# Loading alpha ahead of x, and moving the w_in transposes into the first fills

## The chip, the cores and the metric

The kernel runs on one core of a Trainium2 chip. The metric is the device time in microseconds (us).

## The reference

Two stages follow each other. First an attention block: 32 inducing vectors attend to x (4 batches of 12480 tokens, 128 channels), which gives h; x then attends to h. Then a feed-forward layer with a leaky ReLU that has one slope for each hidden unit:

```python
h = mab(I, x)                 # softmax attention of 32 vectors over 12480 tokens
x = mab(x, h)                 # (4 * 12480, 128)
h = x @ w_in                  # 128 -> 2048
g = np.maximum(h, 0.0) + alpha * np.minimum(h, 0.0)
out = g @ w_out               # 2048 -> 128
```

## The kernel before

The leaky ReLU is split into a ReLU part, with the weights W1 = (1 - alpha) * w_out, and a linear part that needs only the 128 x 128 matrix Amat = w_in @ (alpha * w_out). So alpha is needed to make W1 and AW = alpha * w_out on GpSimd, and w_in must be transposed once (two calls of `w_inT`, eight transposes each) for Amat.

A *fill* is the kernel's unit of steady work: four matmuls `ring<-rep,hW`, four evictions with ReLU to `gt` by ACT or DVE, and sixteen matmuls `acc<-W,gt`. Before the first fill there is a *head* that loads batch 0, transposes x on PE, and computes h. A planner in the kernel chooses for each fill which of ACT and DVE evicts which bank; extra work is given to a slot (group, step) of the fills with `at(...)`.

The head, with cuts. `pin` keeps the program order on an engine; `bank()` takes the next of six PSUM banks.

```python
ind_f = const.tile([M, C], f32, name="ind_f")
nc.sync.dma_start(out=ind_f[:], in_=inducing)
xs = const.tile([P, NQ, GRP], f32, name="xs")           # first block of x
pin(nc.sync.dma_start(out=xs[:, 0:2, :], in_=src[:, 0:2, :]))      # SP half
pin(nc.scalar.dma_start(out=xs[:, 2:4, :], in_=src[:, 2:4, :]))    # ACT half
for u in order[1:3]:
    a_load(st, u, pieces=2)                             # GpSimd queue, casts to bf16
make_identity(nc, ident[:]); make_identity(nc, ident32[:])
al_f = const.tile([KC, P], f32, name="al_f")
nc.sync.dma_start(out=al_f[:], in_=moe_alpha.rearrange("(k p) -> k p", p=P))
for u in order[3:]:
    a_load(st, u, pieces=2)
...                                                     # w_in, w_out on the GpSimd queue
nc.tensor.transpose(alp[:, :KC], al_f[:], ident32[:KC, :KC])
nc.vector.tensor_copy(out=alT[:], in_=alp[:, :KC])
nc.vector.tensor_scalar(out=om_al[:], in0=alT[:], ...)  # 1 - alpha
...
def warm(n):                                            # n transposes that nobody reads
    ...
pin(nc.vector.tensor_copy(out=xn0[:, 0:2, :], in_=xs[:, 0:2, :]))  # the cast of the SP half
pin(nc.scalar.copy(out=xn0[:, 2:4, :], in_=xs[:, 2:4, :]))
a_xpose_pe(st, order[0])                                # PE transposes of x
for i in range(n - 1):
    a_xpose_pe(st, order[i + 1])
    ...                                                 # e1 transposes, scores, accumulation
h_sum(st); w_scale(W1, om_al); w_scale(AW, alT)
...
h_den(st)
w_inT(0)
a_accum(st, order[n - 1], pool)
...                                                     # h, hW, then the fills
at(0, lambda: w_inT(KC // 2), 3, (460, "A", 960))
at(1, w_amat, 1, (950, "D", 250))
```

The softmax here doesn't subtract the row's maximum and nothing guards it: scores larger than these inputs give would overflow.

Of the kernel before, what the change touches and what calls it, by code (L numbers as in the profile page):

```python
# [11 lines left out]
MULT = mybir.AluOpType.mult  # L12
ADD = mybir.AluOpType.add
AXX = mybir.AxisListType.X

P = 128
# [8 lines left out]
def kernel(  # L25
# [9 lines left out]
    nc = tc.nc  # L35
    f32 = mybir.dt.float32
# [12 lines left out]
    KC = DFF // P  # L49
# [38 lines left out]
    def bank():  # L88
        t = ring[ring_n[0] % RING]
        ring_n[0] += 1  # L90
        return t
# [57 lines left out]
    def a_xpose_pe(st, u):  # L149
        xn = st.xn[u]  # L150
        if u < NS:
            for i in range(2):
                tp = bank()[:].bitcast(bf16)
                for k in range(2 * NB):
                    q, j = 2 * i + k // NB, k % NB
                    pin(nc.tensor.transpose(
                        tp[:, k * P : (k + 1) * P], xn[:, q, j * C : (j + 1) * C], ident[:]
                    ))
                dst = st.xT[:, u, 2 * i : 2 * i + 2, :].rearrange("c q t -> c (q t)")
                if i == 0 or u == order[-1]:  # L160
                    pin(nc.vector.tensor_copy(out=dst, in_=tp))
                else:
                    pin(nc.scalar.copy(out=dst, in_=tp))
        else:
            tp = bank()[:].bitcast(bf16)
            for j in range(JR):
                pin(nc.tensor.transpose(
                    tp[:, j * PR : (j + 1) * PR], xn[:, j, :], ident[:PR, :PR]
                ))
            pin(nc.vector.tensor_copy(  # L170
                out=st.xTr[:].rearrange("c j p -> c (j p)"), in_=tp[:, :REM]
            ))

    def e_xpose_pe(st, u):
        e1 = st.e1.pop(u)
        tp = bank()[:].bitcast(bf16)
        if u < NS:
            e1T = work.tile([P, NB, P], bf16, name="e1T", tag="e1T")
            for j in range(NB):
                pin(nc.tensor.transpose(  # L180
                    tp[:, j * P : (j + 1) * P], e1[:, j * P : (j + 1) * P], ident[:]
                ))
            pin(nc.vector.tensor_copy(
                out=e1T[:].rearrange("p j m -> p (j m)"), in_=tp[:, : NB * P]
            ))
        else:
            e1T = work.tile([P, JR, M], bf16, name="e1Tr", tag="e1Tr")
            for j in range(JR):
                pin(nc.tensor.transpose(
                    tp[:PR, j * M : (j + 1) * M], e1[:, j, :PR], ident[:M, :M]  # L190
                ))
            pin(nc.vector.tensor_copy(
                out=e1T[:PR].rearrange("p j m -> p (j m)"), in_=tp[:PR, : JR * M]
            ))
        st.e1T[u] = e1T

    def a_scores(st, u, by_dma=True):
        ps = bank()
        if u < NS:
            for q in range(NQ):  # L200
                mm(ps[32 * q : 32 * q + 32, :], IT[:], st.xT[:, u, q, :])
            e1 = work.tile([P, GRP], bf16, name="e1", tag="e1")
            pin(nc.scalar.activation(
                out=e1[:], in_=ps[:], func=EXP, scale=scale, accum_out=st.es[:, u : u + 1]
            ))
            if by_dma:
                e1T = work.tile([P, NB, P], bf16, name="e1T", tag="e1T")
                pin(nc.sync.dma_start_transpose(out=e1T[:], in_=e1[:]))
        else:
            mm(ps[0:M, :REM], IT[:], st.xTr[:].rearrange("c j p -> c (j p)"))  # L210
            e1 = e1r
            pin(nc.scalar.activation(
                out=e1[:, :, :PR],
                in_=ps[0:M, :REM].rearrange("m (j p) -> m j p", j=JR),
                func=EXP, scale=scale, accum_out=st.es[0:M, u : u + 1],
            ))
            if by_dma:
                e1T = work.tile([P, JR, M], bf16, name="e1Tr", tag="e1Tr")
                pin(nc.sync.dma_start_transpose(
                    out=e1T[:], in_=e1[:].rearrange("m j p -> m (j p)")  # L220
                ))
        if by_dma:
            st.e1T[u] = e1T
        else:
            st.e1[u] = e1
# [3 lines left out]
    def a_accum(st, u, into=None, first=False):  # L229
        xn = st.xn.pop(u)  # L230
        e1T = st.e1T.pop(u)
        alone = into is None
        ps = bank() if alone else into
        if u < NS:
            for j in range(NB):
                for q in range(NQ):
                    mm(
                        ps[32 * q : 32 * q + 32, :C],
                        e1T[:, j, 32 * q : 32 * q + 32],
                        xn[:, q, j * C : (j + 1) * C],  # L240
                        start=(j == 0 and (alone or first)), stop=(j == NB - 1),
                        skip_group_check=not alone,
                    )
            if alone:
                pin(nc.vector.tensor_tensor(
                    out=st.hacc[:], in0=ps[:, :C], in1=st.hacc[:], op=ADD
                ))
        else:
            for j in range(JR):
                mm(  # L250
                    ps[0:M, :C], e1T[:PR, j, :], xn[:, j, :],
                    start=(j == 0 and alone), stop=(j == JR - 1),
                    skip_group_check=not alone,
                )
            if alone:
                pin(nc.vector.tensor_tensor(
                    out=st.hacc[0:M, :], in0=ps[0:M, :C], in1=st.hacc[0:M, :], op=ADD
                ))
# [212 lines left out]
    st = new_batch(0)  # L471
    ind_f = const.tile([M, C], f32, name="ind_f")
    nc.sync.dma_start(out=ind_f[:], in_=inducing)


    xs = const.tile([P, NQ, GRP], f32, name="xs")
# [6 lines left out]
    make_identity(nc, ident[:])  # L483
    ident32 = const.tile([P, P], f32, name="ident32")
    make_identity(nc, ident32[:])
    al_f = const.tile([KC, P], f32, name="al_f")
    nc.sync.dma_start(out=al_f[:], in_=moe_alpha.rearrange("(k p) -> k p", p=P))
    for u in order[3:]:
        a_load(st, u, pieces=2)
    w_in_b = const.tile([C, DFF], bf16, name="w_in_b")  # L490
# [10 lines left out]
    for q in range(4):  # L501
# [13 lines left out]

    e1r = const.tile([M, JR, P], bf16, name="e1r")
    nc.vector.memset(e1r[:], 0.0)
    alp = bank()
    alT = const.tile([P, KC], f32, name="alT")
    nc.tensor.transpose(alp[:, :KC], al_f[:], ident32[:KC, :KC])  # L520
    nc.vector.tensor_copy(out=alT[:], in_=alp[:, :KC])
    om_al = const.tile([P, KC], f32, name="om_al")
    nc.vector.tensor_scalar(
        out=om_al[:], in0=alT[:], scalar1=-1.0, scalar2=1.0, op0=MULT, op1=ADD
    )
    W1 = const.tile([P, KC, C], bf16, name="W1")
    AW = const.tile([P, KC, C], bf16, name="AW")
    winT = const.tile([P, KC, C], bf16, name="winT")
    Amat = const.tile([C, C], bf16, name="Amat")


    def w_scale(dst, fac):
        for j in range(NJ):
            f = fac[:, j::NJ]
            fb = bass.AP(tensor=f.tensor, offset=f.offset, ap=[f.ap[0], f.ap[1], [0, C]])
            pin(nc.gpsimd.tensor_tensor(
                out=dst[:, j::NJ, :], in0=w_out_f[:, j::NJ, :], in1=fb, op=MULT
            ))
# [7 lines left out]
    def w_inT(k0):  # L546
        wtp = bank()[:].bitcast(bf16)
        for k in range(8):
            pin(nc.tensor.transpose(
                wtp[:, k * P : (k + 1) * P],  # L550
                w_in_b[:, (k0 + k) * P : (k0 + k + 1) * P], ident[:],
            ))
        pin(nc.scalar.copy(
            out=winT[:, k0 : k0 + 8, :].rearrange("p k c -> p (k c)"), in_=wtp
        ))
# [15 lines left out]

    pool = accs[0][:, 0, :]
    n = len(order)
    a_xpose_pe(st, order[0])
    for i in range(n - 1):
        a_xpose_pe(st, order[i + 1])
        if i > 0:
            e_xpose_pe(st, order[i - 1])
        a_scores(st, order[i], by_dma=False)
        if 0 < i < n - 2:  # L580
            a_accum(st, order[i - 1], pool, i == 1)
    a_scores(st, order[n - 1], by_dma=False)
    e_xpose_pe(st, order[n - 2])
    a_accum(st, order[n - 3], pool)
    h_sum(st)
    w_scale(W1, om_al)
    w_scale(AW, alT)
    e_xpose_pe(st, order[n - 1])
    a_accum(st, order[n - 2], pool)
    h_den(st)  # L590
    w_inT(0)
    a_accum(st, order[n - 1], pool)
    pin(nc.vector.tensor_copy(out=st.hacc[:], in_=pool))
    warm(6)
# [13 lines left out]
    def at(slot, fn, j=1, cost=None):  # L608
        tasks.setdefault((slot, j), []).append((fn, cost))
# [5 lines left out]
    for q in range(1, NQ):  # L615
        at(0, lambda q=q: b_scores_pe(st, 0, q), q, (240, "A", 480))
    at(1, lambda: b_den_pe(st, 0, 0), 0, (130, "D", 250))
    at(0, lambda: w_inT(KC // 2), 3, (460, "A", 960))
    at(1, w_amat, 1, (950, "D", 250))
    at(1, lambda: h_linear(st), 2, (80, "D", 250))  # L620
# [151 lines left out]
```

## Time and profile before

| | before |
|---|---|
| median time, 3 runs | 597.71 us (597.15 to 598.29) |
| span of the profiled run (an execution of 598.94 us) | 597.2 us |
| SP half of x: issued, landed | 1.20, 6.21 us |
| first x transpose on PE | 8.00 us |
| clock records: full TensorE clock from | 14.53 us |
| last x piece landed | 19.87 us |
| first fill | 28.47 us |

The page of the kernel before; part 1 (busy time, share, instructions) and part 4 (the chain that ended last):

```profile
...
PE 582.9 (98%) x9186; PEld 435.0 (73%) x9186; DVE 518.6 (87%) x878; ACT 507.1 (85%) x994; POOL 84.9 (14%) x170
...
PE 58%; ACT 0%; DVE 0%; issue 0%
...
```

PE is busy nearly all the time, and the chain runs through PE. So what the head loses or gains at the first fill is passed on to the end.

The DVE timeline of the head (start us, duration us, engine, line, operation, tiles):

```profile
...
6.89 0.17 DVE L521 COPY alT<-ring_82 128x16 f32<-128x16 f32 x1 [2.72 <-PE ring_82 L520]
7.10 0.17 DVE L523 TENSOR_SCALAR om_al<-alT 128x16 f32<-128x16 f32 x1
7.18 0.76 DVE L568 CAST xn<-xs 128x1024 bf16<-128x1024 f32 x1
9.07 0.69 DVE L161 COPY xT<-ring_83 128x1024 bf16<-128x1024 bf16 x1 [1.13 <-PE ring_83 L156]
...
```

The cast of x (L568) starts at 7.18, right behind the two alpha instructions. Its data were there earlier, as the view of the tile `xs` shows: the SP queue issued the half at 1.2 us, and the longer of the two landings (the SP half's) took 5.0 us.

```profile
...
L478 SPq DMA_DIRECT2D xs<-in_x_dram x1: 409/409/409, 1.2 to 1.2; - x1
...
DMA to landing us min/median/max: 4.0/4.5/5.0
```

The PE timeline of the head and of the first fill:

```profile
...
6.59 0.26 PE L520 MATMUL ring_82<-ident_110,al_f 16*128 16x16 f32 x1 [2.64 <-DMA al_f<-in_moe_alpha_dram]
8.00 1.04 PE L156 MATMUL ring_83<-ident,xn 128*128 128x128 bf16 x8 [1.14 <-DVE xn L568]
8.82 1.06 PE L156 MATMUL ring_84<-ident,xn 128*128 128x128 bf16 x8
...
14.76 0.62 PE L156 MATMUL ring_85<-ident,xn 128*128 128x128 bf16 x8
...
21.38 0.61 PE L156 MATMUL ring_86<-ident,xn 128*128 128x128 bf16 x8
...
24.80 0.38 PE L94 MATMUL ring_86<-et,fold 128*128 128x1 f32 x2
25.05 0.61 PE L549 MATMUL ring_81<-ident,w_in_b 128*128 128x128 bf16 x8
25.58 0.41 PE L94 MATMUL acc_87<-xn,e1T 128*32 128x128 bf16 x16
...
28.47 0.39 PE L94 MATMUL ring_85<-rep,hW 32*128 32x512 bf16 x1
...
```

Eight x transposes take 1.04 us at first and 0.62 us from 14.76 on: in the trace they start every 107 ns, then every 56 ns. The eight w_in transposes (L549) stand before the last accumulation (25.58).

The table by stretch (length, then busy us of PE, PEld, DVE, ACT, POOL, then clock, DMA share, GB/s) shows the first fills:

```profile
...
30.00:35.00 5.00, 5.00 (x71) 3.65 (x71) 4.47 (x8) 4.80 (x9) 5.00 (x6) 1.00 0.01 3
...
```

In these 5 us PE has no idle time, ACT 0.20 us and DVE 0.53 us. The page's clock column cannot be used for the head: it shows 1.00 where the trace holds no clock record. The switch times in this text come from the trace's clock records, which say from when to when a full or a half clock was granted; they agree with the spacing of the transposes.

### The profile page before, as it was taken

What the parts mean: (1) busy time and instruction counts of PE and PEld (TensorE: products, weight loads), DVE (VectorE), ACT (ScalarE), POOL (GpSimd) and SP (SyncE); (2) the same over time, 40 slices, a digit from 0 to 9 for tenths busy, and PEclk for the clock granted to TensorE, in tenths of its full rate; (3) what the DMA queues carried; (4) which work ended last, traced back from release to release, by engine and by line L of the source; (5) the groups of instructions that cost most, each with busy time, mean ns of one, the idle gap of its engine ahead of it and who ended that gap; (6) DMA issues with size and microseconds to landing.
All of it is one profiled execution on the core that took longest, in us unless ns stands there. A gap on an engine that the chain in (4) does not pass through costs nothing.

```text
span 597.2 us, 21700 instructions
## 1 busy us (share of the span) xinstructions
PE 582.9 (98%) x9186; PEld 435.0 (73%) x9186; DVE 518.6 (87%) x878; ACT 507.1 (85%) x994; POOL 84.9 (14%) x170
## 2 busy tenths in 40 slices
PE   4999999999999999999999999999999999999997
PEld 3677777777777777677777777777777777777775
DVE  2588899889889998899998989988988898998995
ACT  3588888898889888888888988889888889989886
POOL 6331111010111111101011111101011101101100
PEclk9999999999999999999999999999999999999999
DMA  9644799862237669983134478986212221221211
GB/s 197 161 93 103 162 161 176 172 105 85 68 87 147 134 141 173 166 154 112 40 99 120 101 162 157 173 177 103 86 68 80 80 98 57 83 97 56 93 46 61
DMA packets 79009, 69.18 MB, mean 116 GB/s; under 512 B 53200, under 2 KB 68448, under 8 KB 78912
## 3 DMA queue, kind: packets, MB, share of 16 engines
q0 software_dynamic: 12720, 39.30, 26.4%
q1 hardware_dynamic: 66048, 27.97, 24.2%
q8 instruction: 72, 1.18, 0.9%
q10 hardware_dynamic: 144, 0.52, 0.3%
q14 instruction: 25, 0.20, 0.1%
HBM read 39.94 MB, written 28.62 MB: 115 GB/s over the span
## 4 chain that ended last, share of the span: by engine, by line
PE 58%; ACT 0%; DVE 0%; issue 0%
PE acc_88 L94 21%; PE acc_87 L94 21%; PE ring_85 L94 3%; PE ring_83 L94 3%; PE ring_84 L94 3%; PE ring_82 L94 3%; PE ring_81 L94 3%; PE ring_86 L94 3%; ACT gt L405 0%; DVE gt L407 0%; DVE ob L456 0%
## 5 line engine op out<-in xcount | busy, mean ns | idle before, releaser
L94 PEld LDWEIGHTS <-gt 128*128 128x128 bf16 x6272 | 352.4, 98 | 78.9 <-issue 75.9
L94 PE MATMUL acc_87<-W_168,gt 128*128 128x128 bf16 (+1 forms) x3136 | 209.0, 220 | 0.0
L94 PE MATMUL acc_88<-W_168,gt 128*128 128x128 bf16 (+1 forms) x3136 | 208.8, 220 | 0.0
L465 POOL DMA_DIRECT2D out_dram<-ob x99 | 53.7, 542 | 492.8 <-DVE ob L456 422.3
L405 ACT ACTIVATE gt<-ring_83 128x512 bf16<-128x512 f32 (+1 forms) x160 | 95.5, 597 | 10.9 <-ACT gt L405 5.4
L405 ACT ACTIVATE gt<-ring_81 128x512 bf16<-128x512 f32 (+1 forms) x159 | 95.0, 597 | 11.2 <-PE ring_84 L94 5.6
L94 PE MATMUL ring_82<-rep,hW 32*128 32x512 bf16 (+1 forms) x270 | 101.6, 379 | 0.0
L94 PE MATMUL ring_83<-rep,hW 32*128 32x512 bf16 (+1 forms) x270 | 101.1, 378 | 0.0
L94 PE MATMUL ring_85<-rep,hW 32*128 32x512 bf16 (+1 forms) x267 | 100.4, 379 | 0.3 <-ACT gt L405 0.3
L94 PE MATMUL ring_84<-rep,hW 32*128 32x512 bf16 (+1 forms) x266 | 99.6, 378 | 0.8 <-DVE gt L407 0.8
L94 PE MATMUL ring_86<-rep,hW 32*128 32x512 bf16 (+1 forms) x264 | 99.3, 379 | 0.0
L94 PE MATMUL ring_81<-rep,hW 32*128 32x512 bf16 (+1 forms) x263 | 98.9, 379 | 0.0
L405 ACT ACTIVATE gt<-ring_84 128x512 bf16<-128x512 f32 x147 | 88.2, 600 | 12.0 <-ACT gt L405 5.4
L405 ACT ACTIVATE gt<-ring_85 128x512 bf16<-128x512 f32 (+1 forms) x147 | 87.7, 596 | 11.8 <-PE ring_82 L94 5.3
L405 ACT ACTIVATE gt<-ring_86 128x512 bf16<-128x512 f32 (+1 forms) x143 | 85.6, 599 | 12.3 <-ACT gt L405 5.9
L405 ACT ACTIVATE gt<-ring_82 128x512 bf16<-128x512 f32 (+1 forms) x142 | 84.9, 598 | 12.1 <-PE ring_85 L94 4.4
L407 DVE TENSOR_SCALAR gt<-ring_82 128x512 bf16<-128x512 f32 (+1 forms) x123 | 84.2, 684 | 8.5 <-PE ring_84 L94 4.1
L407 DVE TENSOR_SCALAR gt<-ring_86 128x512 bf16<-128x512 f32 (+1 forms) x116 | 79.4, 684 | 12.9 <-PE ring_82 L94 8.4
L407 DVE TENSOR_SCALAR gt<-ring_84 128x512 bf16<-128x512 f32 (+1 forms) x113 | 77.1, 682 | 9.3 <-PE ring_85 L94 3.8
L407 DVE TENSOR_SCALAR gt<-ring_85 128x512 bf16<-128x512 f32 x115 | 78.9, 686 | 7.1 <-PE ring_81 L94 2.5
L407 DVE TENSOR_SCALAR gt<-ring_83 128x512 bf16<-128x512 f32 x104 | 71.4, 687 | 9.4 <-PE ring_85 L94 4.4
L407 DVE TENSOR_SCALAR gt<-ring_81 128x512 bf16<-128x512 f32 x99 | 68.0, 687 | 6.8 <-PE ring_82 L94 2.3
(321 smaller groups left out, 372.1 us busy)
## 6 DMA issues: line engine op xcount, KB each, us to landing
out_dram<-ob POOLq DMA_DIRECT2D x96, 256.0 KB, 2.8
rep<-e2d SPq DMA_DIRECT2D x92, 128.0 KB, 3.0
xn<-in_x_dram POOLq DMA_DIRECT2D x18, 512.0 KB, 6.2
xn<-in_x_dram POOLq DMA_DIRECT2D x10, 256.0 KB, 8.9
w_out_f<-in_moe_w_out_dram POOLq DMA_DIRECT2D x1, 1024.0 KB, 13.9
xs<-in_x_dram ACTq DMA_DIRECT2D x1, 512.0 KB, 4.0
xs<-in_x_dram SPq DMA_DIRECT2D x1, 512.0 KB, 5.0
w_in_b<-in_moe_w_in_dram POOLq DMA_DIRECT2D x1, 512.0 KB, 11.9
```

The costliest lines, as they stand in the source:

```text
L94: return pin(nc.tensor.matmul(o, lhsT, rhs, start=start, stop=stop, **kw))
L405: pin(nc.scalar.activation(out=gt[:, r, :w], in_=ps[:, :w], func=RELU))
L407: pin(nc.vector.tensor_relu(gt[:, r, :w], ps[:, :w]))
L465: pin((nc.sync if last_one else nc.gpsimd).dma_start(out=dst, in_=ob[:pp, :nb, :]))
```

## The change

The intent: alpha arrives early, so that its transpose and its two DVE instructions no longer stand before x's cast; they go into the third step of the head, where DVE has time. Sixteen warm transposes fill PE's wait for x. The first eight w_in transposes leave the head for slot 0 of the fills.

```diff
     nc.sync.dma_start(out=ind_f[:], in_=inducing)
+    al_f = const.tile([KC, P], f32, name="al_f")
+    nc.sync.dma_start(out=al_f[:], in_=moe_alpha.rearrange("(k p) -> k p", p=P))
 ...
-    al_f = const.tile([KC, P], f32, name="al_f")
-    nc.sync.dma_start(out=al_f[:], in_=moe_alpha.rearrange("(k p) -> k p", p=P))
 ...
-    (alpha transpose, alT copy, om_al: at once, ahead of the cast of x)
+    def factors():
+        (the same three instructions, pinned)
 ...
+    warm(8)
+    warm(8)
     a_xpose_pe(st, order[0])
     for i in range(n - 1):
         a_xpose_pe(st, order[i + 1])
         if i > 0:
             e_xpose_pe(st, order[i - 1])
+        if i == 2:
+            factors()
 ...
-    a_accum(st, order[n - 3], pool)
     h_sum(st)
     w_scale(W1, om_al)
     w_scale(AW, alT)
+    a_accum(st, order[n - 3], pool)
     e_xpose_pe(st, order[n - 1])
     a_accum(st, order[n - 2], pool)
     h_den(st)
-    w_inT(0)
+    warm(4)
     a_accum(st, order[n - 1], pool)
 ...
+    at(0, lambda: w_inT(0), 2, (460, "A", 960))
     at(0, lambda: w_inT(KC // 2), 3, (460, "A", 960))
```

More of the change, by code (lines that the diff above doesn't have):

```diff
@@ L517 @@
     nc.vector.memset(e1r[:], 0.0)
-    alp = bank()
     alT = const.tile([P, KC], f32, name="alT")
-    nc.tensor.transpose(alp[:, :KC], al_f[:], ident32[:KC, :KC])
-    nc.vector.tensor_copy(out=alT[:], in_=alp[:, :KC])
     om_al = const.tile([P, KC], f32, name="om_al")
-    nc.vector.tensor_scalar(
-        out=om_al[:], in0=alT[:], scalar1=-1.0, scalar2=1.0, op0=MULT, op1=ADD
-    )
     W1 = const.tile([P, KC, C], bf16, name="W1")
@@ L529 @@
     Amat = const.tile([C, C], bf16, name="Amat")
+    def factors():
+        alp = bank()
+        pin(nc.tensor.transpose(alp[:, :KC], al_f[:], ident32[:KC, :KC]))
+        pin(nc.vector.tensor_copy(out=alT[:], in_=alp[:, :KC]))
+        pin(nc.vector.tensor_scalar(
+            out=om_al[:], in0=alT[:], scalar1=-1.0, scalar2=1.0, op0=MULT, op1=ADD
+        ))
     def w_scale(dst, fac):
```

## The prediction

> **What bounds the kernel now.** PE is busy 98% of the 597.2 us span and carries the chain that ended last; DVE has 87%, ACT 85% (page, parts 1 and 4). From about 28.5 us on, fills follow one another, about 1.4 us each. The change touches only the head before them and the first fills. A shorter head should shift the rest one to one, no more.
>
> **The head now (timeline, DMA landings).** The SP half of x's first block lands at 6.21 us, but DVE casts it only at 7.18: its in-order queue first waits for the alpha transpose, which waits for alpha landing at 6.46. PE starts the x transposes at 8.00. They issue every 107 ns until about 14.4, then every 56 ns: PE begins at half rate. From 14.4 on it runs 1.0 to 1.5 us behind the x loads: the last x piece lands at 19.87, its transposes start at 21.38. The DMA engines are full up to 24 us. Then a serial tail (scores, e1 transpose, accumulation, h, hW), in which w_in transposes at 25.05 delay the last accumulation by about 0.54 us; first fill at 28.47.
>
> **What the change does.**
> 1. Alpha no longer stands before the cast. SP issues x 0.45 us later. In the packets, SP's x starts only at 3.71, as ACT's half ends, so the landing should stay near 6.2 to 6.6. Cast at 6.3 to 6.7, PE start at 7.1 to 7.5: gain 0.5 to 0.9 us.
> 2. Sixteen warm transposes fill PE's wait from about 4.0 to 5.7 us. [...] 30% chance that the fast rate comes clearly earlier. [...] Even so, the last x landing caps the gain up to there at about 1.4 us.
> 3. Four warm transposes (0.22 us) replace eight w_in transposes (0.54 us) before the last accumulation: gain 0.3 us.
> 4. The w_in transposes go into slot 0 of the fills: PE 0.54 us, ACT 1.0 us. There (30 to 35 us) PE has 5.00 of 5.00, ACT 4.80, DVE 4.47. Loss 0.5 to 0.8 us.
> 5. The factors in the third step: 0.05 us PE, 0.3 us DVE, hidden. The earlier place of the scaling on POOL gives nothing: w_out lands at 26.34, the scaling starts at 26.51, AW ends at 34.6, before its use.
> 6. The eviction plan changes: a few tenths, either sign.
>
> **Sum.** Head −1.0 to −1.8 (first fill at about 27.2), fills +0.6: net −0.8 us. From 597.71 to about 596.9; range 595.5 to 598.1. Chances: faster by over 2% 0.01, within 2% 0.98, slower by over 2% 0.01.
>
> **What would show it.** DVE cast at 6.3 to 6.7; first x transpose at 7.1 to 7.5; the switch to 56 ns still after 10.5 us; last x landing near 19.9; first fill near 27.2; POOL scaling still at about 26.5; first fills about 0.6 us longer in sum; steady fills unchanged.
>
> **What would make it wrong.** The alpha load could delay the x half on its queue[...], which eats step 1. The fast rate could come at a random time and move single runs by up to 1 us. A worse eviction plan could cost 1 us over 400 fills; or the first fills could wait for W1.

The sum came to a net gain of 0.8 us (597.71 to about 596.9): 1.0 to 1.8 us off the head, 0.6 us onto the fills. Points 1 and 3 give 0.8 to 1.2 us of the head's gain; the rest was not itemised, and only an earlier clock (point 2) is named beside them. "Full up to 24 us" is a DMA share of 0.97 to 1.13 in each two microseconds from 4 to 24 us of the kernel before.

## The result, and the profile after

The changed kernel took 600.96 us (median of 6 runs, 599.90 to 602.02), against 597.58 us (6 runs, 597.15 to 598.29) for the kernel before. The ratio of the fast runs is 1.0057 (95% interval 1.0044 to 1.0070). A ratio is the mean time of one kernel's fast runs over that of the other's fast runs of the same rounds, so it is not quite the ratio of the medians. The change costs about 3.4 us where 0.8 us of gain was forecast.

The page after:

```profile
...
PE 584.7 (97%) x9206; PEld 436.6 (73%) x9206; DVE 518.7 (86%) x878; ACT 506.9 (85%) x994; POOL 84.7 (14%) x170
...
PE 93%; DMA 3%; ACT 1%; SPq 1%; DVE 1%; issue 0%; DVEq 0%; ACTq 0%
...
```

The PE share goes from 98% to 97%. The chain that ended last could be followed further here and now includes a share for the load of `xs`.

The DVE timeline after:

```profile
...
9.46 0.69 DVE L570 CAST xn<-xs 128x1024 bf16<-128x1024 f32 x1 [5.31 <-DMA xs<-in_x_dram]
...
18.34 0.17 DVE L528 COPY alT<-ring 128x16 f32<-128x16 f32 x1
18.55 0.17 DVE L529 TENSOR_SCALAR om_al<-alT 128x16 f32<-128x16 f32 x1
...
```

The alpha instructions did go to 18.3 us, out of the way, as intended. But the cast starts at 9.46, not at 6.3 to 6.7. The view of the tile `xs` says why:

```profile
...
L480 SPq DMA_DIRECT2D xs<-in_x_dram x1: 415/415/415, 1.7 to 1.7; - x1
...
DMA to landing us min/median/max: 3.9/5.8/7.8
```

The SP half was issued at 1.7 us (1.67 in the trace) and took 7.8 us to land, at 9.43. Issued 0.47 us later, it landed 3.22 us later. The PE timeline after:

```profile
...
3.87 1.89 PE L546 MATMUL acc<-ident 128*128 128x128 bf16 x16
10.21 1.89 PE L156 MATMUL ring<-ident,xn 128*128 128x128 bf16 x16 [4.46 <-DVE xn L570]
...
16.92 1.07 PE L156 MATMUL ring<-ident,xn 128*128 128x128 bf16 x16
...
27.04 0.38 PE L94 MATMUL ring<-et,fold 128*128 128x1 f32 x2
27.28 0.38 PE L546 MATMUL acc<-ident 128*128 128x128 bf16 x4
27.60 0.41 PE L94 MATMUL acc<-xn,e1T 128*32 128x128 bf16 x16
...
30.48 0.77 PE L94 MATMUL ring<-rep,hW 32*128 32x512 bf16 x6
...
```

The sixteen warm transposes end before 6 us and PE then idles for 4.46 us. The first x transpose comes at 10.21 (8.00 before), the first fill at 30.48 (28.47 before): 2.02 us lost. The tail behind `h_den` is shorter, as forecast: from the `et,fold` matmuls to the last accumulation it is 0.56 us here and 0.78 us before.

The first fills after, in the PE timeline:

```profile
...
33.80 0.61 PE L551 MATMUL ring<-ident,w_in_b 128*128 128x128 bf16 x8
...
36.20 0.61 PE L551 MATMUL ring<-ident,w_in_b 128*128 128x128 bf16 x8 [0.25 <-ACT winT L555]
...
```

The second group of w_in transposes waits 0.25 us for the ACT copy of the first. From the first fill to the start of the eleventh the changed kernel takes 17.38 us against 16.57: another 0.81 us. Beyond that, the fills of the two traces keep their distance to 0.01 us over long stretches, except for one wait of about 1.2 us in each, at different places (the last section returns to it). At the last fill the distance is 2.98 us. Over the seventeen traces of this text, PE waits of 0.9 to 1.8 us for a late DMA stand behind the head in seven, at different places, and in none of the other ten. So they move single executions by over 1 us, of either kernel: the profiled execution of the kernel before, which has one, took 598.94 us, 1.2 us above the median.

### The profile page after: what moved, and what is told of

Same layout as the page of the kernel before. It is cut to its first block, busy times and chain, and to the rows that moved or that the text cites. A ratio compares the mean times of both kernels' runs of the same rounds, so it can differ in the third digit from the quotient of the medians.

```text
span 599.9 us, 21742 instructions
## 1 busy us (share of the span) xinstructions
PE 584.7 (97%) x9206; PEld 436.6 (73%) x9206; DVE 518.7 (86%) x878; ACT 506.9 (85%) x994; POOL 84.7 (14%) x170
## 4 chain that ended last, share of the span: by engine, by line
PE 93%; DMA 3%; ACT 1%; SPq 1%; DVE 1%; issue 0%; DVEq 0%; ACTq 0%
PE acc L94 65%; PE ring L94 26%; DMA rep<-e2d 2%; DMA xs<-in_x_dram 1%; PE ring L156 1%; ACT gt L405 1%; SPq L139 1%; DVE xT L161 0%; PE ring L180 0%; SPq L327 0%; DVE e1T L183 0%; PE acc L546 0%; ACT xT L163 0%; ACT winT L555 0%; DVE xn L570 0%
## 5 line engine op out<-in xcount | busy, mean ns | idle before, releaser
L405 ACT ACTIVATE gt<-ring 128x512 bf16<-128x512 f32 x898 | 468.8, 598 | 70.4 <-PE ring L94 29.0
L407 DVE TENSOR_SCALAR gt<-ring 128x512 bf16<-128x512 f32 x670 | 435.7, 685 | 54.9 <-PE ring L94 41.5
L94 PE MATMUL acc<-W,gt 128*128 128x128 bf16 x6272 | 417.8, 220 | 0.0
L94 PE MATMUL ring<-rep,hW 32*128 32x512 bf16 (+1 forms) x1600 | 158.2, 379 | 1.2 <-DMA rep<-e2d 0.9
L94 PEld LDWEIGHTS <-hW 32*128 32x128 bf16 x1600 | 41.3, 91 | 43.1 <-DMA rep<-e2d 1.2
L456 DVE TENSOR_TENSOR ob<-acc,rd 128x512 f32<-128x512 f32 x96 | 65.4, 682 | 2.5 <-PE acc L94 2.5
L94 PEld LDWEIGHTS <-rep 32*128 32x128 bf16 (+2 forms) x408 | 16.2, 94 | 6.3 <-issue 0.9
L94 PE MATMUL acc<-hA,rep 32*128 32x128 bf16 x392 | 19.8, 214 | 0.0
L203 ACT ACTIVATE e<-ring 128x512 bf16<-128x512 f32 x24 | 14.5, 602 | 1.9 <-PE ring L94 1.9
L125 POOL DMA_DIRECT2D xn<-in_x_dram x28 | 15.2, 547 | 3.6 <-DMA xn<-in_x_dram 2.9
L309 ACT ACTIVATE e<-ring 128x512 bf16<-128x512 f32 x23 | 14.1, 612 | 0.0
```

The costliest lines, as they stand in the source:

```text
L94: return pin(nc.tensor.matmul(o, lhsT, rhs, start=start, stop=stop, **kw))
L125: pin(nc.gpsimd.dma_start(out=xn[:, i * w : (i + 1) * w, :], in_=src[:, i * w : (i + 1) * w, :]))
L203: pin(nc.scalar.activation(out=e1[:], in_=ps[:], func=EXP, scale=scale, accum_out=st.es[:, u : u + 1]))
L309: pin(nc.scalar.activation(out=e2[:], in_=ps[:], func=EXP, scale=scale))
L405: pin(nc.scalar.activation(out=gt[:, r, :w], in_=ps[:, :w], func=RELU))
L407: pin(nc.vector.tensor_relu(gt[:, r, :w], ps[:, :w]))
```

## The experiments

The first theory was: *the alpha load costs x its turn at the DMA engines.* The rival was: *the w_in transposes in the fills, with the new eviction plan, cost nearly all.* All results in one table. The columns are read from the profiled run of each kernel in us: issue and landing of x's SP half, first x transpose on PE, switch to the full clock (clock records), last x piece landed, first fill, and the time from the first fill to the start of the eleventh. The ratio is to the kernel before on the same chip.

| kernel | x issue | x landed | x on PE | clock | last x | first fill | ten fills | ratio (95%) |
|---|---|---|---|---|---|---|---|---|
| before | 1.20 | 6.21 | 8.00 | 14.53 | 19.87 | 28.47 | 16.57 | 1 |
| changed | 1.67 | 9.43 | 10.21 | 15.98 | 20.87 | 30.48 | 17.38 | 1.0057 (1.0044 to 1.0070) |
| k1 | 1.67 | 8.13 | 8.91 | 12.51 | 21.90 | 28.97 | 16.57 | 1.0019 (1.0004 to 1.0034) |
| k2 | 1.21 | 6.85 | 7.62 | 12.36 | 20.28 | 27.41 | 17.38 | 1.0002 (0.9985 to 1.0019) |
| k3 | 1.20 | 6.10 | 7.96 | 14.38 | 20.12 | 28.16 | 17.38 | 1.0015 (1.0000 to 1.0030) |
| k4 | 1.20 | 6.09 | 6.86 | 12.84 | 20.72 | 27.79 | 16.83 | 0.9985 (0.9969 to 1.0002) |
| k7 | 1.65 | 8.70 | 9.47 | 14.54 | 21.02 | 29.43 | 17.38 | 1.0045 (1.0031 to 1.0059) |
| k6 | 1.67 | 7.94 | 8.72 | 12.59 | 21.81 | 28.66 | 17.38 | 1.0039 (1.0026 to 1.0051) |
| k8 | 1.66 | 8.69 | 9.46 | 13.48 | 21.41 | 29.07 | 16.57 | 1.0032 (1.0018 to 1.0047) |
| k9 | 1.66 | 8.00 | 8.77 | 13.94 | 21.50 | 28.77 | 17.38 | 1.0033 (1.0019 to 1.0047) |
| k10 | 1.61 | 8.46 | 10.27 | 14.39 | 21.64 | 29.92 | 16.57 | 1.0042 (1.0018 to 1.0066) |
| k11 | 1.65 | 6.91 | 7.74 | 11.30 | 23.19 | 30.61 | 17.38 | one look, 602.11 us |
| k14 | 1.66 | 7.91 | 8.69 | 15.18 | 21.43 | 28.99 | 17.38 | one look, 598.94 us |
| k5 | 1.21 | 6.16 | 7.26 | 9.85 | 20.60 | 27.67 | 16.84 | 0.9983 (0.9970 to 0.9996) |
| k12 | 0.76 | 6.10 | 7.72 | 12.07 | 20.84 | 27.91 | 16.57 | 0.9999 (0.9984 to 1.0014) |
| k13 | 1.20 | 5.90 | 11.45 | 8.55 | 20.24 | 30.23 | 16.83 | one look, 600.20 us |
| k15 | 1.20 | 5.89 | 7.17 | 7.05 | 20.28 | 27.35 | 16.83 | 0.9988 (0.9974 to 1.0001) |

All kernels gave correct results.

### The parts alone: k1, k2, k3, k4

k1 is the kernel before with the alpha load ahead of x.

```diff
     nc.sync.dma_start(out=ind_f[:], in_=inducing)
+    al_f = ...; nc.sync.dma_start(out=al_f[:], in_=moe_alpha...)
 ...
-    al_f = ...; nc.sync.dma_start(out=al_f[:], in_=moe_alpha...)
```

> The kernel before, with the alpha load put ahead of x on the sync queue and nothing else changed. Queue theory (the alpha load costs the SP half of x its turn at the DMA engines): x's SP half lands near 9.4 us instead of 6.2, the first x transpose starts near 10.2 instead of 8.0, first fill near 30.5, time 2 us or more above before, about 599.7. Rival (the w_in transposes in the fills and the new eviction plan cost nearly all): x lands near 6.6, time within 0.5 us of before.

Measured: x landed at 8.13, the first x transpose came at 8.91, the first fill 0.50 us later than before, ratio 1.0019 (about 1.1 us). The direction is the first theory's, the size half of what it expected. In this profiled run the full clock came early (12.51), and it was the last x piece that set the first fill: it landed at 21.90, 2.03 us later than before, and the first fill came 7.07 us after it, as in the kernels further below whose head is bound by x's transfers. So a late x half may cost time in two ways, at the start of the transposes and at the last piece.

k2 is the changed kernel with the alpha load back behind x.

```diff
     nc.sync.dma_start(out=ind_f[:], in_=inducing)
-    al_f = ...; nc.sync.dma_start(out=al_f[:], in_=moe_alpha...)
 ...
     make_identity(nc, ident32[:])
+    al_f = ...; nc.sync.dma_start(out=al_f[:], in_=moe_alpha...)
```

> The changed kernel, with only the alpha load put back behind x on the sync queue. Queue theory: x's SP half lands near 6.2, DVE casts it at once (6.3), first x transpose near 7.1, first fill near 27.3; the fills still cost about 0.85 more, so about 597.3, some 3 us below the changed kernel. Rival: first fill may be early, but the time stays 2 us or more above before (near 600).

Measured: x landed at 6.85, the cast started at 6.87, first fill at 27.41, median 597.24 us, ratio 1.0002. Taking back this one line takes back the whole loss (the first fill comes early enough to pay for the longer first fills, 17.38 us here too). As the main cause, the rival falls here; k3 shows what its part is worth.

k3 is the kernel before with the first eight w_in transposes in the fills.

```diff
     h_den(st)
-    w_inT(0)
+    warm(4)
 ...
+    at(0, lambda: w_inT(0), 2, (460, "A", 960))
```

> The kernel before, with only the first eight w_in transposes moved into slot 0 of the fills, four warm transposes in their old place. Queue theory: first fill about 0.3 us earlier (28.15), first fills up to slot 1 about 0.85 us longer, so net +0.5 us, about 598.1. Rival: +2 us or more.

Measured: first fill 0.31 us earlier, the first ten fills 0.81 us longer (17.38 against 16.57), so a net loss of 0.50 us in the trace; ratio 1.0015. This part moves work from a place where it cost 0.3 us to one where it costs 0.8 us.

k4 is the changed kernel with both parts undone: alpha behind x, w_in in the head.

```diff
     (as k2)
 ...
-    warm(4)
+    w_inT(0)
     a_accum(st, order[n - 1], pool)
 ...
-    at(0, lambda: w_inT(0), 2, (460, "A", 960))
```

> The changed kernel with alpha behind x and the first eight w_in transposes back in the head: only the later factors and the 16 warm transposes are left of the change. Queue theory: first x transpose near 7.1 and first fill near 27.6, 0.9 us before the 28.47 of the kernel before, fills as before: about 596.7, the first to beat it. Rival theory (plan): no different from before within 0.5 us.

Measured: cast at 6.11 at once on landing, first x transpose at 6.86, first fill at 27.79, median 596.78 us against 597.37, ratio 0.9985 (0.9969 to 1.0002), a gain that is not clear of noise. So the idea that the alpha instructions stood before the cast was right, as the trace shows; the load order that came with it was the trouble.

### Once more on one chip, and the warm transposes: k7, k6

k7 is the changed kernel, unedited.

> The changed kernel once more, beside its own variants on one chip. In the first set, the alpha place alone cost 1.2 us and the w_in place alone 0.9 us, while the whole change cost 3.4 us on another occasion. If the parts add up: about 2 us above before, x's SP half landing between 8 and 9.5 us. If the parts make each other worse: again about 3.4 us above before.

Measured: x landed at 8.70, ratio 1.0045, about 2.7 us. The two parts' ratios (1.0019 and 1.0015) add up to about 2.0 us, and in this run's trace the eleventh fill starts 1.77 us later than before; both lie below 2.7, but within the widths of the intervals. So that the parts make each other worse is not shown. How late x lands differs from trace to trace (7.9 to 9.4 us), and so does the clock.

k6 is the changed kernel without its first sixteen warm transposes.

```diff
-    warm(8)
-    warm(8)
     a_xpose_pe(st, order[0])
```

> The changed kernel without its 16 warm transposes. Theory that they are useless, since PE idles again before x is cast: same time as the changed kernel on this chip within 0.5 us. Rival theory (they help the clock): about 1 us slower, the fast rate later. Second rival (they make the alpha order worse): faster by 1 us or more.

Measured: 599.84 us against 600.26 of k7, on the same chip; the intervals of the ratios overlap. If the sixteen transposes help or hurt, it is too little to tell here.

### What makes x late: k8, k10, k9, k14, k11

k8 was meant to make x late without putting alpha ahead of it.

```diff
+    pin(nc.vector.memset(xs[:, 0:1, :], 0.0))
     pin(nc.sync.dma_start(out=xs[:, 0:2, :], in_=src[:, 0:2, :]))
```

> The kernel before, alpha behind x as there, but the sync queue's x load is made about half a microsecond late by a VectorE memset of part of the tile that it fills. If the lateness of x against the GpSimd loads is the cause: x's SP half lands at 8 us or later, time about +1 us. If it is the small alpha load standing ahead of x in the same queue: x lands near 6.5, cast near 7.3, first x transpose near 8.1, time as before.

The trial missed its aim: the alpha load was not pinned, so it was issued at 1.21 us while x waited for the memset. It became a second sample of alpha ahead (x landed at 8.69, ratio 1.0032). k10 repeats it with the alpha load pinned behind x.

```diff
+    pin(nc.vector.memset(xs[:, 0:1, :], 0.0))
     pin(nc.sync.dma_start(out=xs[:, 0:2, :], in_=src[:, 0:2, :]))
 ...
-    nc.sync.dma_start(out=al_f[:], in_=moe_alpha...)
+    pin(nc.sync.dma_start(out=al_f[:], in_=moe_alpha...))
```

> The same trial as the one before of x made late by a memset, where the program order had slipped and alpha went ahead; now alpha is held behind x, so that the sync queue has only the inducing load ahead of x and x is issued near 1.66 us. Lateness alone as the cause: x's SP half lands at 8 us or later, with a few of its 16 engines far behind the others. The small alpha load ahead as the cause: x lands between 6.1 and 6.9, all 16 engines close together.

The tile `xs` in k10 (the memset, the issue on SP, and the landings):

```profile
...
L478 DVE MEMSET xs<- x1: 485/485/485, 1.1 to 1.1; 128x512 f32 x1
L479 SPq DMA_DIRECT2D xs<-in_x_dram x1: 355/355/355, 1.6 to 1.6; - x1
...
DMA to landing us min/median/max: 3.9/5.4/6.8
```

Issued at 1.6 us with only the inducing load ahead of it, as in the kernel before, x took 6.8 us to land, at 8.46; ratio 1.0042. (The ratio counts more than the landing: alpha landed at 8.81, and the cast stood behind its two instructions until 9.53.) So the first theory falls in its literal form. An alpha load ahead in the queue is not needed for the delay. It is enough that x is issued 0.4 to 0.5 us later. Over all seventeen traces: eight had x issued by 1.21 us and it landed between 5.89 and 6.85; eight had it issued between 1.61 and 1.67 beside GpSimd's loads and it landed between 7.91 and 9.43; the one left is k11, below.

The DMA packets show what being late means. The 16 DMA engines report x's landing one by one. In the kernel before, all 16 reports came between 5.51 and 6.21 us. In the changed kernel eleven came between 5.95 and 6.43 and the other five at 6.92, 7.12, 7.72, 7.86 and 9.43. In the kernel before, the first data packet of the GpSimd queue started at 5.16 us, when x's SP half was nearly through. In the changed kernel it started at 3.53 us, before x's SP half (3.92). So in this trace GpSimd's first load had come in ahead. After that, the last x packets (4 KB) came singly among GpSimd's packets (2 KB), the last five of them from 7.46 to 8.74 us, one every 0.32 us.

So the packets of the SP and the GpSimd queue interleave here, and 0.47 us of issue time went with 3.22 us of landing.

So the second theory: *x, when late, loses to GpSimd's first loads.* k9, k14 and k11 are the changed kernel with those loads issued later. k9 puts the identities ahead of them, which made them only 0.38 us later (1.66).

```diff
-    for u in order[1:3]:
-        a_load(st, u, pieces=2)
     make_identity(nc, ident[:]); make_identity(nc, ident32[:])
+    for u in order[1:3]:
+        a_load(st, u, pieces=2)
```

> The changed kernel, alpha ahead of x, but GpSimd makes the identities before it issues its first x loads, so that these come about 1 us later. If x loses its turn to GpSimd's loads: x's SP half lands near 6.3, cast near 6.4, first x transpose near 7.2, and the time falls by 1 us or more against the changed kernel, although the x stream starts later. If the alpha load alone costs the time: x still lands at 8 us or later.

Measured: x landed at 8.00, thirteen of the 16 engines by 6.35 and three at 7.31, 7.93 and 8.00. Expectation missed.

k14 puts the pick memsets ahead of them too (first load issued at 2.19, half a microsecond after x).

```diff
+    (pick and its five memsets)
+    for u in order[1:3]:
+        a_load(st, u, pieces=2)
```

> The changed kernel, alpha ahead of x, with GpSimd's first loads behind the identities and the five pick memsets, near 2.2 us instead of 1.28, so clearly behind x's issue at 1.66. If x's place against GpSimd's loads decides: x's SP half lands between 6.1 and 6.9, all 16 engines close together. If it does not: at 8 us or later, with a few engines far behind.

```profile
...
L480 SPq DMA_DIRECT2D xs<-in_x_dram x1: 415/415/415, 1.7 to 1.7; - x1
...
DMA to landing us min/median/max: 3.9/5.1/6.3
```

Measured: x landed at 7.91, with seven of the 16 engines between 6.79 and 7.91. Expectation missed again: who is issued first does not decide it. Nor does whose data come first. GpSimd's first data packet started at 5.25 us here, no earlier than in the kernel before (5.16); still 32 of the 128 packets of x's SP half started after 6.0 us, and none did in the kernel before.

k11 holds all of GpSimd's loads back behind its fold work (first issue at 4.89).

```diff
+    (fold, pick)
+    for u in order[1:3]:
+        a_load(st, u, pieces=2)
+    for u in order[3:]:
+        a_load(st, u, pieces=2)
+    (w_in, w_out)
```

> The changed kernel, alpha ahead of x, with all of GpSimd's loads held back until after its identity and fold work, about 4 us later; diagnostic only, the x stream then ends about 3 to 4 us later and the time rises by about as much. If x loses to GpSimd's loads: x's SP half lands by 6.2 us, all 16 engines close together, alpha ahead or not. If the alpha load delays x by itself: x still lands at 8 us or later.

```profile
...
L480 SPq DMA_DIRECT2D xs<-in_x_dram x1: 414/414/414, 1.7 to 1.7; - x1
...
DMA to landing us min/median/max: 4.1/4.7/5.3
```

Measured: x took 5.3 us and landed at 6.91, thirteen engines by 6.09 and three between 6.80 and 6.91. GpSimd's first data packet started at 6.26. So with GpSimd out of the way most of the delay is gone, but not all: 6.91 is 0.70 us above the kernel before. What holds a few engines back even then is not settled. What is shown is that x issued by 1.21 us did not meet it in any of eight traces (the nearest is k2, with one engine at 6.85 and fifteen by 5.94). That GpSimd's data make it worse rests on this one trace. (Its clock also fell back to half from 18.13 to 21.54 us, so its first fill is not compared.)

### Do transposes release the clock? k13

k13 has 96 warm transposes in place of 16, alpha behind x, w_in in the head.

```diff
-    warm(8)
-    warm(8)
+    for _ in range(12):
+        warm(8)
```

> Diagnostic: 96 warm transposes, alpha behind x. From about 3.9 us on PE does nothing but transposes, up to about 14 us at the slow rate. If transposes count for the clock: the switch to the fast rate falls inside this block[...]. If only other matmuls count: all 96 run at 107 ns and the switch comes after the first score matmuls, at 16 us or later.

Busy PE and its matmul count in three stretches of two us, all inside the block of transposes (the clock column holds its default here):

```profile
...
4.00:6.00 2.00, 2.00 (x21) 1.00 1.05 327
6.00:8.00 2.00, 2.00 (x21) 1.00 1.06 165
9.00:11.00 2.00, 2.00 (x39) 1.00 1.12 210
...
```

21 transposes reach into two microseconds at first, 39 later on; the block starts at 3.9 us and ends at 11.45. The clock records put the switch at 8.55, in the middle of the block. So transposes count: from 3.9 us to the switch PE had run nothing else (`warm` issues `nc.tensor.transpose`). In the kernels with at most 16 warm transposes the switch came between 3.6 and 6.5 us after the first x transpose, and in k13, k5 and k15 4.7, 6.0 and 3.2 us after the start of the warm block.

### A version that beats both? k5, k15, k12

k5, and k15 which is the same file on another chip, are k4 with 32 warm transposes, so that PE works without a break from 3.9 us until x is there.

```diff
-    warm(8)
-    warm(8)
+    for _ in range(4):
+        warm(8)
```

> Alpha behind x, w_in transposes in the head, and 32 warm transposes instead of 16, so that PE works without a break from about 4 us to the first x transpose near 7.3. If transposes count for the clock: the fast rate comes [...]before or early in the x transposes, instead of 12.4 to 14.8; PE then waits for the x pieces, and first fill comes near last x landing plus 7 us, 27 to 27.5. Time near 596.3, at most 0.5 us better than with 16. If transposes do not count: the fast rate comes at 12 us or later, as before.

> The variant with alpha behind x, 32 warm transposes and all w_in transposes in the head, again, on whatever chip comes. If its gain is real: ratio to before near 0.998, first fill 7.1 us after the last x landing. If not: within 0.0005 of 1.

Measured: switch to the full clock at 9.85 and 7.05 us, first fill at 27.67 and 27.35. Medians 596.91 us against 597.97 (ratio 0.9983, 0.9970 to 0.9996) and 596.60 against 597.43 (0.9988, 0.9974 to 1.0001). One interval lies just below 1 and the other just includes it, and k4 with 16 transposes had 0.9985: a gain of 0.1 to 0.2% over the kernel before is likely, one over k4 is not shown. The PE timeline of k15:

```profile
...
3.88 3.46 PE L546 MATMUL acc<-ident 128*128 128x128 bf16 x32
7.17 1.06 PE L156 MATMUL ring<-ident,xn 128*128 128x128 bf16 x16
...
17.78 0.62 PE L156 MATMUL ring<-ident,xn 128*128 128x128 bf16 x8 [0.76 <-DMA xn<-in_x_dram]
...
27.35 0.77 PE L94 MATMUL ring<-rep,hW 32*128 32x512 bf16 x6
...
```

In k15 the x transposes run at the full rate from the first one (16 in 1.06 us), but at 17.78 PE waits for a piece of x to land. In k1, k4, k5, k12 and k15 alike the first fill comes exactly 7.07 us after the last x landing (in k2, 7.13; in the kernel before, 8.60). Once the clock is early enough, the head is bound by x's transfers, and a faster PE gains nothing more.

k12 issues x first on the sync queue and moves the inducing load behind ACT's half; the w_in transposes are in the head, and there are no warm transposes before x's.

```diff
-    nc.sync.dma_start(out=ind_f[:], in_=inducing)
     pin(nc.sync.dma_start(out=xs[:, 0:2, :], in_=src[:, 0:2, :]))
     pin(nc.scalar.dma_start(out=xs[:, 2:4, :], in_=src[:, 2:4, :]))
+    pin(nc.scalar.dma_start(out=ind_f[:], in_=inducing))
+    (alpha, pinned, on sync)
 ...
-    warm(8)
-    warm(8)
```

> Alpha behind x and w_in transposes in the head, no warm transposes, and x's SP half first in its queue, with the inducing load moved to the scalar queue behind its x half. Queue theory: both x halves land near 5.5, the first x transpose near 6.4, first fill near 27.5, where the last x landing (near 20) caps it; time near 596.4. If x landing early is worth nothing: first fill near 28 and the time as before within 0.5 us.

Measured: x landed at 6.10, not 5.5; with the SP half issued at 0.76 us instead of 1.20, the ACT half lands at 5.82 instead of 4.7. The cast began only at 6.98, because the inducing load (landed at 6.31) and its own cast stood ahead of it on DVE: the same mistake as alpha's in the kernel before. Ratio 0.9999.

## Why the prediction was wrong

The forecast was a gain of 0.8 us, range 595.5 to 598.1; measured 600.96. Point by point:

1. **The step that failed** was in point 1: "In the packets, SP's x starts only at 3.71, as ACT's half ends, so the landing should stay near 6.2 to 6.6". It landed at 9.43, and at 7.9 to 8.7 in the repeats with alpha ahead (k11, which holds GpSimd back, apart). The first x transpose moved from 8.00 to 10.21 (9.47 in k7) instead of to 7.1 to 7.5, so the head's term of the sum, a gain of 1.0 to 1.8 us, became a loss of 2.02 (0.96 in k7). The start did keep its place behind ACT's half: the SP half's first packet came at 3.92 us, against 3.71. What the reasoning missed is the time from there to the last engine's landing: 5.5 us instead of 2.5. That GpSimd's loads were issued at 1.28, just after x's 1.20, and that their data had waited until 5.16, could have been a warning; but k14 shows that neither order, of issue or of data, is the whole story, and why a few engines fall behind stays open. The prediction named a late x as a risk, but as the work of an alpha load on x's queue; k10 shows that no alpha load ahead of it is needed, only the later issue (1.61 us, landed at 8.46).
2. The rest of point 1 was right: with alpha's instructions off DVE's queue, the cast starts at once when x lands (k2 6.87 after 6.85, k4 6.11 after 6.09). In the kernel before it had waited 0.97 us behind them (6.21 to 7.18).
3. Point 2 was right in its estimate: sixteen transposes with an idle stretch after them brought no early clock (15.98 in the changed kernel, 14.54 in k7; 12.59 in k6, without them), the likelier case, by the 30%. That transposes count was right too, but it took k13 to show it (8.55, inside its block): in the trace of before, about a quarter of PE's busy time up to the switch was other matmuls. The prediction named a random time of the switch as a risk of up to 1 us for single runs; the switch fell between 11.3 and 16.0 us in the fourteen traces with at most 16 warm transposes.
4. Point 3 was right: 0.3 us forecast, 0.31 in k3.
5. Point 4 was right, at its edge: 0.5 to 0.8 us forecast, 0.81 measured in all eight traces that have the w_in transposes in the fills. Points 3 and 4 together already made this half of the change a loss of 0.5 us.
6. Point 5 was right: the factors run at 18.3 to 18.7 us on DVE, and PE's next wait for DVE was 0.26 us against 0.19 at that step of the kernel before; the scaling on GpSimd started at 26.92, just behind w_out's landing at 26.75.
7. Point 6 was right: after the eleventh fill the traces keep their distance to 0.01 us over long stretches.
8. The cap was right: x's transfers bound the head once the clock is early (first fill 7.07 us after the last x landing in k1, k4, k5, k12 and k15). It did not bind the changed kernel, whose first fill came 9.61 us after the last x landing. But that landing, forecast near 19.9, came at 20.87: it lay between 20.9 and 21.9 in the eight traces with x issued late beside GpSimd's loads, and between 19.9 and 20.8 in the eight with x issued by 1.21.

In the profiled runs the sum is: 2.02 us at the first fill (head), 0.81 us in the first ten fills, 0.15 us after them, 2.98 us at the last fill. These are two executions; k7, the same changed kernel, lost 0.96 us at the first fill (x landed at 8.70, the full clock came at 14.54) and the same 0.81 in the first ten. The medians' 3.4 us is thus not taken apart to the last half microsecond. The mechanism of the gain was right, worth about 0.7 us at the first fill in k4 (28.47 to 27.79, with a clock that also came earlier); the price of the load order was missed.

## What to carry to other kernels

When a load is moved on its queue, look at what else is issued within the same microsecond on the other queues: here, half a microsecond made a load of 5 us one of 6 to 8, whichever of the two was issued first, and the load was through only with the slowest of its 16 engines (in the changed kernel eleven by 6.43 us, the last at 9.43). To free an engine from waiting for a small operand, as DVE's cast stood 0.97 us behind alpha's instructions, move the instructions that consume it, and leave the load behind the large one (k4: the cast 0.02 us after x landed). Work taken out of a head needs a new place with idle time on the engines that it uses: k3 saved 0.31 us in the head and lost 0.81 in fills where PE had none.

## What else the traces show

- What the issue time can cost: 0.4 to 0.5 us later cost 1.7 to 3.2 us of landing beside GpSimd's loads, because a few of the 16 engines (two in k8, seven in k14) ended far behind the rest.
- A load can land late in the middle of a kernel too. In the trace of before, four copies of `rep` were issued on SP from 232.53 to 234.05 us; the first three landed after 2.6 to 3.4 us, the fourth, issued as the issue of a 512 KB load on GpSimd's queue ended (233.51 to 234.05), after 8.24 us, and PE waited:

```profile
...
PEld L94 <- DMA rep<-e2d: 1.1, 1, 1.1
...
```

  The changed kernel has such a wait of the same size near 386 us instead. Nobody varied this, so its cause is argued from the packets of the head, not shown.
- The clock column of the profile page can read full speed where no clock record exists: in the kernel before it read 1.00 up to 14.5 us while transposes ran every 107 ns.
